# Moving the query transposes, one query load and one value fold inside the queues of a pooled-attention and maxout-FFN kernel

## The chip, the core and the metric

The kernel runs on one core of a Trainium2 chip. The metric is the device time of one execution in microseconds (us). The profile's own clock begins with the first instruction of the span; all times "at 62.28" below are on that clock.

## The reference

```python
# q, k, v: (8 batches, 8 heads, 576 tokens, 64), float32
k_p = k.reshape(B, H, 72, 8, D).mean(axis=3)      # keys and values pooled by 8
v_p = v.reshape(B, H, 72, 8, D).mean(axis=3)
scores = scale * np.matmul(q, k_p.transpose(0, 1, 3, 2))
attn = softmax(scores)                            # exp, divided by the sum
x = np.matmul(attn, v_p)                          # then (8 * 576, 512)
h = np.maximum(np.maximum(x @ w1, x @ w2), x @ w3)   # w: 512 x 768
out = h @ w_out                                   # 4608 x 512, float32
```

## The kernel before

Two kinds of units run side by side. The attention goes by batch: b = 0 to 7, 576 tokens each. The feed-forward part goes by tile of 512 tokens: n = 0 to 8. Since 576 is not 512, the tile n needs rows of two batches: the hidden products of tile 3 need the first three chunks of 128 tokens of batch 3, those of tile 4 the rest of batch 3 and the first two chunks of batch 4, those of tile 5 the rest of batch 4 and the first two chunks of batch 5.

The order of the work is written out by hand. Inside a `manual_schedule`, each engine and each queue does its instructions in the order in which the program records them. `block(n, plan, parts)` records tile n as a row of slots: each slot is one piece of `hidden(n)` (line L335, products with the two stored weight differences) or of `project(n)` (lines L380 and L384, then a copy to `osb` at L389 and two stores by SP at L393). For tiles 2 to 4 the slots 0 to 11 are hidden pieces and 12 to 19 are project pieces. After a slot's own piece, the plan's steps of the attention for that slot are recorded by `do(b, steps)`:

- `k`: the pooled keys `kp` are turned on TensorE (L176) and copied into `kz` (L181).
- `s0` to `s7`: the scores of one head (L194) and their exponentials (L199). They read the turned queries `qT`.
- `v0` to `v4`: the values of one chunk of 128 tokens (L243), and their division by the sums (L249, L251) into `xn`.
- `x0` to `x4`: `xn` is turned into `xT`, which the feed-forward products read. For batches 0 to 2 TensorE does it (L233); from batch 3 on it is a transposing DMA that SP issues (L227).
- `T`: the queries of a whole batch are turned from `qb` into `qT` by one transposing DMA that SP issues (L277). It is used from batch 3 on; batches 0 to 2 are turned on TensorE (L169). Below, T(b) is the one of batch b, and x(b,c) is the transpose of chunk c of batch b.

SP's queue thus holds, in one order, the stores of `project`, the x transposes and the T transposes. An instruction in it that waits holds everything behind it.

POOL (GpSimd) issues all loads of k, v and q from batch 1 on, and it folds k and v: three additions each, from eight rows to one (L138, L139, L141). `pool_work(n)` is recorded at slot 0 of block n. It first issues the loads of batch n + 3, the load of k made to wait for a matmul of that slot by `after(...)`, and then does the folds that `FOLDS_OF[n]` lists. The folds `k2` and `v2` stand between blocks 0 and 1. A load into `qb` waits for the transpose that read the buffer before: the load of q of batch 4 waits for T(3), that of batch 6 for T(4), that of batch 7 for T(5).

Each tag has few buffers: `qb`, `vt` and the later `kt` have two, `qT` has two, `xn` six and `osb` five.

After block 5, `weave()` does the tiles 6 to 8 in another form (products `pA`, `pB`, `pC` at L712) with the scores and values of batches 6 and 7 between them, by a list `ORDER`; its first step turns the keys of batch 7.

Of the kernel before, what the change touches and what calls it, by code (L numbers as in the profile page):

```python
# [14 lines left out]
def kernel(  # L15
# [51 lines left out]
    def after(loads, first):  # L67
        for x in loads:
            tc.add_manual_dep(x.ins, first.ins.name, mybir.DependencyInfo(
                mybir.DependencyClass.Sync, mybir.DependencyReason.DATA),  # L70
                reason="weights first")

    def load_k(b, eng, dtype=F16, parts=1):
        kts[b] = (const if b == 0 else ld).tile([96, 6, POOL, D], dtype,
                                                name=f"kt{b == 0}", tag=f"kt{b == 0}")
        src = k[b].rearrange("h s d -> (h s d)").rearrange(
            "(p i j d) -> p i j d", p=96, i=6, j=POOL)
        n = 6 // parts
        return [eng.dma_start(out=kts[b][:, i:i + n], in_=src[:, i:i + n])
                for i in range(0, 6, n)][-1]  # L80

    def load_v(b, eng, dtype=F16, cuts=(0, H)):
        vts[b] = ld.tile([Sp, H, POOL, D], dtype, name="vt", tag="vt")
        src = v[b].rearrange("h (sp j) d -> sp h j d", j=POOL)
        return [eng.dma_start(out=vts[b][:, h:g], in_=src[:, h:g])
                for h, g in zip(cuts, cuts[1:])][-1]

    def load_q(b):
        qbs[b] = ld.tile([128, 4, NG, D], BF16, name="qb", tag="qb")
        src = q[b].rearrange("h s d -> (h s d)").rearrange(  # L90
            "(hp p t d) -> p hp t d", hp=4, p=128, t=NG)
        n = 2 if b == 0 else 4
        for i in range(0, 4, n):
            nc.gpsimd.dma_start(out=qbs[b][:, i:i + n], in_=src[:, i:i + n])
# [51 lines left out]
    def fold_k(b, e, i0=0, i1=6):  # L146
        if b not in kps:
            new_kp(b)
        fold(e, kts[b][:, i0:i1], kps[b][:, i0:i1], F16 if e is nc.vector else F32)

    def fold_v(b):
        fold(nc.gpsimd, vts[b], vp_all[:, b, :, 0:D])
# [327 lines left out]
    def block(n, plan, parts, folds=()):  # L480

        for slot, _ in enumerate(part for stage in parts for part in stage(n)):
            if slot == 0 and n > 0:
                pool_work(n, mms[-1])
            for b, steps in plan.get(slot, ()):
                if b < B:
                    do(b, steps)
            if folds and slot in FOLDS:
                next(folds.pop(0))
# [14 lines left out]
    def plan1():  # L504
        return {1: [(1, "x2")], 2: [(1, "v4")], 3: [(1, "x3")],
                5: [(1, "x4")],
                6: [(2, "k")], 7: [(2, "q0")], 9: [(2, "q1")], 11: [(2, "q2 s0")],
                12: [(2, "s1 q3")], 13: [(2, "s2")], 14: [(2, "s3")], 15: [(2, "s4")],
                16: [(2, "s5")], 18: [(2, "s7")],
                19: [(2, "v0")],  # L510
                20: [(2, "v1 x0")], 21: [(2, "v2 x1")], 22: [(2, "v3 x2")],
                23: [(2, "v4 x3")], 24: [(2, "x4"), (4, "T")], 17: [(2, "s6"), (3, "T")]}

    def plan(n):
        b = n + 1
        got = {0: [(b, "k")]}
        got.update({2 + h: [(b, f"s{h}")] for h in range(H)})
        got.update({12 + c: [(b, f"v{c} x{c}")] for c in range(5)})
        got[18] = [(b + 2, "T")]
        return got  # L520

    FOLDS_OF = {1: "k3 v3", 2: "k4 v4 k5", 3: "v5 k6", 4: "v6 k7 v7"}

    def pool_work(n, mm):

        if n + 3 < B:
            after([load_k(n + 3, nc.gpsimd)], mm)
            load_v(n + 3, nc.gpsimd)
            load_q(n + 3)
        for name in FOLDS_OF.get(n, "").split():  # L530
            if name[0] == "k":
                fold_k(int(name[1]), nc.gpsimd)
            else:
                fold_v(int(name[1]))
# [227 lines left out]
    def with_keys(n):  # L762
        got = plan(n)
        got[17] = got.get(17, []) + [(n + 2, "k")]
        return got

    folds = [f for wi in range(1, 3) for f in [fold_w(wi)] * 4]
    block(1, plan1(), (hidden, project))
    for n in range(2, 5):
        block(n, with_keys(n) if n == 5 - 1 else plan(n),  # L770
              (hidden, project))
# [50 lines left out]
```

The softmax here doesn't subtract the row's maximum and nothing guards it: scores larger than these inputs give would overflow.

## Time and profile before

| | us |
|---|---|
| median of 3 runs | 234.96 |
| lowest and highest of them | 231.76, 235.74 |
| the profiled execution | 231.92 |
| its span in the profile | 230.2 |
| TensorE (PE) busy in the span | 220.2 |
| POOL busy | 137.9 |
| DVE busy | 128.2 |
| ACT busy | 120.9 |

The profiled execution is one of those near the lowest time. The 1.7 us between its time and its span lie outside the first and the last instruction. An engine's busy time does not count the issuing of DMAs on SP; POOL's issuing of a load, 0.55 to 0.86 us each, is shown in the timeline of POOL. A DMA has two times: how long the issuing queue is held, and when the data has landed, which the trace gives by the semaphores.

### The profile page before, as it was taken

The page shows a single profiled execution, that of the slowest core. Times are in us where ns is not written, and L with a number is a line of the kernel's source. Part 1 is how long each engine was busy: PE and PEld are TensorE (multiplying, and loading weights), DVE is VectorE, ACT ScalarE, POOL GpSimd, SP SyncE. Part 2 cuts the span into 40 slices and gives each one's busy share as a digit, 9 for nine tenths or more (in the row PEclk, how much of TensorE's full clock was granted, in tenths as well). Part 3 has the DMA queues.
Part 4 walks back from the last instruction along what each step waited for, and adds up shares of the span by engine and source line. Part 5 has one row for each costly group of instructions (what it writes and reads, how often), then busy time and mean ns, then how long its engine had stood idle before and what let it go on. Part 6 is the DMA issues. An engine that isn't in the chain of part 4 may idle for free.

```text
span 230.2 us, 4549 instructions
## 1 busy us (share of the span) xinstructions
PE 220.2 (96%) x1766; PEld 137.1 (60%) x1766; DVE 128.2 (56%) x238; ACT 120.9 (53%) x216; POOL 137.9 (60%) x113
## 2 busy tenths in 40 slices
PE   7688999999999999999999999999999999999992
PEld 2466745558756455545554555455678667786682
DVE  3558867037425333633362336278579887897730
ACT  2257534755874577237623762574686535465330
POOL 7665201999927999999995999900243442920020
PEclk9999999999999999999999999999999999999999
DMA  6999999999499889979995999691430536302236
GB/s 180 207 195 197 212 202 211 177 187 219 91 186 165 199 164 167 152 171 184 197 201 119 171 182 223 120 192 33 91 66 17 117 72 99 74 20 46 68 73 182
DMA packets 47173, 33.53 MB, mean 146 GB/s; under 512 B 27312, under 2 KB 41904, under 8 KB 47152
## 3 DMA queue, kind: packets, MB, share of 16 engines
q0 software_dynamic: 16960, 16.98, 46.0%
q1 hardware_dynamic: 30032, 16.13, 32.3%
q8 instruction: 14, 0.23, 0.4%
q10 hardware_dynamic: 160, 0.13, 0.2%
q14 instruction: 7, 0.06, 0.1%
HBM read 34.60 MB, written 9.44 MB: 191 GB/s over the span
## 4 chain that ended last, share of the span: by engine, by line
PE 89%; DMA 4%; DVE 2%; issue 1%; ACT 1%; POOL 1%; POOLq 0%; DVEq 0%
PE pw L335 27%; PE po L384 18%; PE po L380 12%; PE pA L712 7%; PE psc L194 5%; PE pav L243 4%; DMA vt<-in_v_dram 4%; PE pC L712 3%; PE pm L322 2%; PE oA L649 2%; PE pB L712 2%; PE pxt L233 1%; PE pkt L176 1%; DVE xn L251 1%; PE oC L649 1%
## 5 line engine op out<-in xcount | busy, mean ns | idle before, releaser
L335 PE MATMUL pw<-xT,mw 128*128 128x512 f16 (+1 forms) x336 | 73.1, 349 | 0.3 <-ACT xT L237 0.2
L384 PE MATMUL po<-mwo,hT 128*128 128x512 f16 (+1 forms) x198 | 46.8, 372 | 0.0
L343 DVE TENSOR_TENSOR hT<-t,pw 128x512 f16<-128x512 f16 (+1 forms) x42 | 25.5, 609 | 37.2 <-ACT et L199 22.6
L389 ACT COPY osb<-po 128x512 f32<-128x512 f32 (+1 forms) x32 | 18.5, 580 | 42.2 <-PE po L384 40.1
L335 PEld LDWEIGHTS <-mw 128*128 128x128 f16 x336 | 29.0, 98 | 19.5 <-DVE mw L308 0.6
L199 ACT ACTIVATE et<-psc 72x576 f16<-72x576 f32 (+2 forms) x54 | 35.2, 661 | 6.6 <-PE psc L194 6.6
L138 POOL TENSOR_TENSOR half<-vt 72x2048 f32<-72x2048 f16 x7 | 28.4, 4061 | 13.9 <-DMA vt<-in_v_dram 13.6
L380 PE MATMUL po<-wm,xT 128*128 128x512 f16 (+1 forms) x132 | 33.1, 373 | 0.0
L341 ACT ACTIVATE t<-pw 128x512 f16<-128x512 f32 (+1 forms) x42 | 22.6, 537 | 14.8 <-PE pw L335 13.1
L251 DVE TENSOR_TENSOR xn<-pav,rcp 128x512 f16<-128x512 f32 x40 | 27.6, 691 | 1.4
L384 PEld LDWEIGHTS <-hT 128*128 128x128 f16 x198 | 18.4, 98 | 16.2
L139 POOL TENSOR_TENSOR half<-half 72x1024 f32<-72x1024 f32 (+1 forms) x13 | 27.3, 2097 | 1.0
L194 PEld LDWEIGHTS <-kz 128*128 128x128 bf16 x191 | 17.5, 98 | 13.7 <-DVE kz L181 0.4
L194 PE MATMUL psc<-qT,kz 128*128 128x320 bf16 (+2 forms) x168 | 22.4, 246 | 0.4 <-DVE kz L181 0.3
L243 PEld LDWEIGHTS <-et 72*128 72x128 f16 x320 | 15.4, 98 | 7.6 <-issue 0.4
L718 ACT CAST pad<-pA 128x512 f16<-128x512 f32 x27 | 15.3, 587 | 8.5 <-PE pA L712 6.0
L138 POOL TENSOR_TENSOR half<-ktFalse 96x1536 f32<-96x1536 f16 x6 | 18.6, 3096 | 0.3
L249 DVE RECIPROCAL rcp<-pav 128x8 f32<-128x8 f32 x40 | 8.2, 206 | 18.4 <-PE pav L243 18.2
L380 PEld LDWEIGHTS <-xT 128*128 128x128 f16 x132 | 11.9, 98 | 9.0
L243 PE MATMUL pav<-vp,et 72*128 72x65 f16 x320 | 16.9, 194 | 0.2 <-ACT et L199 0.2
L693 DVE SCALAR_TENSOR_TENSOR hT<-pad 128x512 f16<-128x512 f16 x18 | 14.4, 810 | 1.8 <-ACT pad L722 1.4
L712 PEld LDWEIGHTS <-sw 128*128 128x128 f16 x144 | 13.7, 98 | 2.7
(102 smaller groups left out, 273.9 us busy)
## 6 DMA issues: line engine op xcount, KB each, us to landing
out_dram<-osb SPq DMA_DIRECT2D x62, 128.0 KB, 2.5
ktFalse<-in_k_dram POOLq DMA_DIRECT2D x7, 576.0 KB, 6.8
qb<-in_q_dram POOLq DMA_DIRECT2D x7, 576.0 KB, 13.6
vt<-in_v_dram POOLq DMA_DIRECT2D x7, 576.0 KB, 11.4
mw<-in_moe_w_dram POOLq DMA_DIRECT2D x9, 256.0 KB, 9.4
ktTrue<-in_k_dram SPq DMA_DIRECT2D x3, 384.0 KB, 4.9
mwo<-in_moe_w_out_dram POOLq DMA_DIRECT2D x1, 768.0 KB, 13.1
qb<-in_q_dram POOLq DMA_DIRECT2D x2, 288.0 KB, 8.2
```

The source lines that it names most:

```text
L138: e.tensor_tensor(out=f, in0=t[:, :, 0:4, :], in1=t[:, :, 4:8, :], op=ALU.add)
L139: e.tensor_tensor(out=f[:, :, 0:2, :], in0=f[:, :, 0:2, :], in1=f[:, :, 2:4, :], op=ALU.add)
L194: nc.tensor.matmul(out, kz_all[b % 2][:, f % 2, h, :], qTs[b][:, n + i0:n + i1, 64 * (h % 2):64 * (h % 2) + 64], start=True, stop=True)
L199: nc.scalar.activation(out=out, in_=in_, func=FT.Exp, scale=1.0 / 64.0)
L243: nc.tensor.matmul(pav[:, h // 4, 65 * (h % 4):65 * (h % 4) + 65], ets[b][:, h, c0:c0 + 128], vp_all[:, b, h, :], start=True, stop=True)
L251: nc.vector.tensor_tensor(out=xn, in0=pv[:, :, :, 0:D], in1=rcp.to_broadcast([128, 2, 4, D]), op=ALU.mult)
L335: mm = nc.tensor.matmul(pw, w_sb[wi][:, kc, bass.ts(jc, 128)], xT[:, kc, col], start=(kc == 0), stop=(kc == KCH - 1))
L341: nc.scalar.activation(out=t, in_=pw, func=FT.Relu)
L343: nc.vector.tensor_tensor(out=hT[:, jc, c0:c1], in0=t, in1=pw, op=ALU.max)
L380: nc.tensor.matmul(po, xT[:, kc, bass.ts(m, 128)], wm_sb[:, kc, c], start=(kc == 0), stop=False)
L384: nc.tensor.matmul(po, hT[:, jc, bass.ts(mm, 128)], wo_sb[:, jc, c], start=False, stop=(jc == JCH - 1))
L712: mm = nc.tensor.matmul(p[:, w], a[:, kc, bass.ts(g, 128)], b[:, kc, :], start=(i in FIRST and w + kc == 0), stop=(w + kc == 2), skip_grou ...
```

## The change

Three things are moved; nothing is added or taken away.

- T moves in the plans. T(3) is recorded at slot 15 of block 1 in place of slot 17. T(5), T(6) and T(7) were recorded at slot 18 of blocks 2, 3 and 4; now T(5) is recorded at slot 14 of block 2, behind x(3,2), and T(6) and T(7) at slot 13 of blocks 3 and 4, behind x(4,1) and x(5,1). T(4) keeps its slot.
- The load of q of batch 4 (the fifth batch) is issued ahead of the loads of k and v of that batch.
- The fold of v of batch 6 is done at the end of block 3's pool work, and so ahead of the loads of batch 7, which stand at the head of block 4's.

```diff
 def plan1():
         ...
-                12: [(2, "s1 q3")], 13: [(2, "s2")], 14: [(2, "s3")], 15: [(2, "s4")],
+                12: [(2, "s1 q3")], 13: [(2, "s2")], 14: [(2, "s3")], 15: [(2, "s4"), (3, "T")],
         ...
-                23: [(2, "v4 x3")], 24: [(2, "x4"), (4, "T")], 17: [(2, "s6"), (3, "T")]}
+                23: [(2, "v4 x3")], 24: [(2, "x4"), (4, "T")], 17: [(2, "s6")]}

 def plan(n):
         ...
-        got[18] = [(b + 2, "T")]
+        got[14 if n == 2 else 13].append((b + 2, "T"))
         return got

-    FOLDS_OF = {1: "k3 v3", 2: "k4 v4 k5", 3: "v5 k6", 4: "v6 k7 v7"}
+    FOLDS_OF = {1: "k3 v3", 2: "k4 v4 k5", 3: "v5 k6 v6", 4: "k7 v7"}

 def pool_work(n, mm):
         if n + 3 < B:
+            if n == 1:
+                load_q(4)
             after([load_k(n + 3, nc.gpsimd)], mm)
             load_v(n + 3, nc.gpsimd)
-            load_q(n + 3)
+            if n > 1:
+                load_q(n + 3)
```

The recorded order on SP changes accordingly, and by nothing else. T(3) has the same place in SP's queue at either slot, since SP has no other instruction between them.

## The prediction

> **What bounds the kernel now.** I read the page's busy times and slices first, then the busy times by stage, then the waits of PE, then the timelines of POOL and SP in the stages that the change touches.
>
> ```profile
> PE 220.2 (96%) x1766; PEld 137.1 (60%) x1766; DVE 128.2 (56%) x238; ACT 120.9 (53%) x216; POOL 137.9 (60%) x113
> ...
> PE   7688999999999999999999999999999999999992
> ...
> PEclk9999999999999999999999999999999999999999
> DMA  6999999999499889979995999691430536302236
> ```
>
> PE is busy for 96% of the span at the full granted clock. What is missing lies at the two ends. The DMA engines are nearly full until slice 26 (about 150 us), so a transfer there takes as long as its neighbours allow.
>
> The busy times by stage (length, then PE, PEld, DVE, ACT, POOL, clock, DMA share, GB/s) show the blocks 2, 3 and 4:
>
> ```profile
> 78.70:101.50 22.80, 22.80 (x160) 11.80 (x158) 9.37 (x17) 11.28 (x19) 22.16 (x13) 1.00 0.92 164
> 101.50:124.30 22.80, 22.80 (x160) 11.80 (x158) 9.37 (x17) 11.28 (x19) 21.13 (x12) 1.00 0.92 177
> 124.30:147.50 23.20, 23.20 (x165) 12.03 (x164) 10.11 (x18) 11.91 (x20) 21.14 (x11) 1.00 1.01 177
> ```
>
> PE has no idle time in them, POOL very little. The waits of PE between 23 and 216 us are one row of 0.2 us:
>
> ```profile
> PE pw L335 <- ACT xT L237: 0.2, 1, 0.2
> ```
>
> So in this execution nothing that the change touches holds PE. Its parts can only move margins: how long before PE needs a thing it is there.
>
> The timeline of POOL at the loads of batch 4, and at those of batch 7 (start, length, in brackets the idle time before and what ended it):
>
> ```profile
> 63.24 0.57 POOL L79 DMA_DIRECT2D ktFalse<-in_k_dram  x1
> 63.80 0.85 POOL L85 DMA_DIRECT2D vt<-in_v_dram  x1
> 70.11 0.78 POOL L94 DMA_DIRECT2D qb<-in_q_dram  x1 [5.45 <-DMA qT<-qb]
> 70.91 3.11 POOL L138 TENSOR_TENSOR half<-ktFalse 96x1536 f32<-96x1536 f16 x1
> ...
> 125.45 0.55 POOL L79 DMA_DIRECT2D ktFalse<-in_k_dram  x1 [2.25 <-PE pw L335]
> 126.00 0.86 POOL L85 DMA_DIRECT2D vt<-in_v_dram  x1
> 127.20 0.78 POOL L94 DMA_DIRECT2D qb<-in_q_dram  x1 [0.35 <-issue]
> ```
>
> POOL stands 5.45 us in the load of q(4) until T(3) is done, with the fold of k(3) behind it. SP's timeline from block 4:
>
> ```profile
> 127.81 9.67 SPq L277 DMA_TRANSPOSE qT<-qb  x1
> 137.59 1.18 SPq L393 DMA_DIRECT2D out_dram<-osb  x2
> 139.31 1.19 SPq L227 DMA_TRANSPOSE xT<-xn  x1
> ```
>
> T(6) holds SP for 9.67 us. The trace has its data landed 14.2 us after its start; T(4), with no load beside it, took 4.0 us and T(3), issued just before two loads, 7.3 us. So a T beside loads is slow, and all behind it on SP waits.
>
> **The change part by part.** Landings are read from the trace's semaphores.
>
> *q(4) ahead of k(4) and v(4).* The load waits for T(3), issued at 62.28 in both kernels, as soon as q(3) has landed (62.14). If T(3) is as quick as T(4) with the two loads no longer beside it, it lands at 66.3; if they did not slow it, at 69.5 as now. From landing to issue took 0.57 us (69.54 to 70.11). Then come 0.78 + 0.57 + 0.85 us of issues: the fold of k(3) starts at 69.1 or 72.3, in place of 70.91. I take 69.1, since the only difference between T(3) and T(4) that the rows show is the loads. The fold takes 6.06 us (70.91 to 76.97), so the keys are there at 75.1 (or 78.4); PE reaches their transposes at 79.55. The margin goes from 2.6 to 4.4 us (or 1.2). On the path: nothing. Without the cover it would be whatever exceeds that margin. k(4) and v(4) land some 4 to 6 us later (71.4 and 75.2 before), but POOL folds them only from about 85 on. T(4) no longer waits for q(4) (2.9 us of SP before 80.63); its first reader is at 104.4, 20 us later.
>
> *T(5) behind x(3,2).* q(5) landed at 98.32, x(3,2) was issued until 98.83, so T(5) issues without a wait. It adds its 2.2 us of SP ahead of two stores, x(3,3) and x(3,4), which landed by 103.85 and are read at 124.1. x(3,2) itself, which landed at 100.44 for a product at 101.36, has the same place: its margin of 0.9 us stays, or grows, if the loads of batch 5 run 1.8 us earlier with POOL. Nothing on the path.
>
> *T(6) behind x(4,1).* q(6) landed at 120.08 (118.3 with POOL's 1.8 us); x(4,1) was issued until 120.24, so T(6) follows without a wait and ahead of the loads of batch 7. I give it 4.0 us, the far bound is 14.2. It is read at 148.2, so either fits. SP pays 2.2 us in block 3 and gets back 9.67 us in block 4, where x(5,0) was issued only 0.5 us after SP had its stores done (139.31 against 138.77). x(4,2) to x(4,4) go 2 to 4 us later, and are read at 147.4. Nothing on the path.
>
> *v(6) folded ahead of the loads of batch 7.* The fold (128.00 to 135.84) fills the 2.25 us in which POOL waited for PE. k(6) was folded by 123.20, or 121.4 with the gain above; plus 7.8 us the loads start at 129.2, not 125.45. At their old times to landing (6.6, 11.6, 13.7) k(7) lands at 135.8, v(7) at 141.4 and q(7) at 144.4. POOL idles 4.4 us, starts k(7) at 135.9 as before, and PE turns the keys at 160.3. T(7) waits on SP from about 143.2 to 144.4 and holds two stores and x(5,2) behind it; that one belongs to tile 6, whose products begin at 163.1, and T(7)'s data is read at 164.9.
>
> What comes nearer is x(5,1). Hidden(5) reads it at 147.37; it landed at 144.99, 3.1 us after its issue. Now q(7) is still loading then. From the rows, an x took 2.4 us with nothing beside it and 5.1 us (x(3,0)) in the tail of batch 5's loads, so it lands between 144.3 and 147.0. I take 146, as its neighbour x(5,0) took 4.4 beside loads: margin 1.4 in place of 2.4 us. On the path nothing, but the thinnest cover of the change.
>
> The Trainium skill, "DMA: Bandwidth & Descriptors", section "Rules for kernel authors", speaks against this part: a DMA should be issued early and waited for late, and two of the three moves issue loads later. The trace has the load of k(7) used 3.9 us after it landed and its keys needed 18 us after the fold. By the rule the loads' delay of 3.8 us would be lost, 235.7 for the profiled execution; by the rows nothing is.
>
> *T(3) at slot 15:* same place on SP and on PE. Nothing.
>
> **The sum.** Removed from PE's path 0, added 0: 231.92 for an execution like the profiled one. The median, 234.96, is 3.0 us over it, and no trace shows where. Either the 3.0 us are of a kind that the change cushions (T(6) only 2.9 us longer, the 0.5 and 2.4 us above, makes PE wait; 6 us longer explains 3.0), or they lie elsewhere. I take the first, since T's times spread from 4.0 to 14.2 us, wider than any transfer that the change leaves alone: 232.0.
>
> **The rivals.** *The 3 us lie outside: 235.0.* The nearest place is the load of v(1): it landed at 39.31, its fold starts at 39.39, and behind it POOL folds k(2), there at 55.39 for PE at 56.48. That margin of 1.1 us is smaller than those that the change widens, and the change does not touch it. Against it: v(1) would have to land 4.1 us later to cost 3.0.
>
> *Batch 7's loads catch x(5,0) and x(5,1): slower.* T(6) lost 10.2 us (14.2 less 4.0) beside these loads. If x(5,0), issued at 139.3, lost as much, it would land at 151.9 and x(5,1) after it at about 153; PE would stand 5.7 us at 147.4, 240.7 on top of the median. It decides from 147.4 on. Against it: x(3,0) lost only 2.7 us in such a tail.
>
> *Faster by over 2%.* PE's idle before 23 us is out of reach, so below 231 there is little to win; it would take both a kernel before at its upper end (235.74) and one after at 231.0. I price it at 230.2.
>
> **How the numbers follow.** The forecast has 0.43, the outside cause 0.32, the loads on x(5,1) 0.14, faster 0.11. A difference under 2% is about what a measurement of this kernel can tell from no change, so the first two, at 1.3% and 0%, are both "within": 0.75. The range runs from 230.6, where half of the faster case begins, over the first two to 236.8, the upper rival's 235.0 with the scatter of the runs (235.74) and a late x(5,1) of 1 us.
>
> **What would show it.** Right: POOL's wait before q(4) at about 3.6 us counted from 63.2, the k(3) fold starting near 69; T(5), T(6) and T(7) each landing in 4 to 6 us, and no SP entry near 9.7 us; PE without idle from 23 us on. Wrong: T(3) still landing near 69.5; idle time of PE at 147.4 ended by xT; or a median near 235, with the idle ahead of block 2.

## The result, and the profile after

The changed kernel has a median of 231.93 us (231.74 to 232.10, 4 runs), and the kernel before, with one run more than shown above, 233.36 us (231.4 to 235.74). The ratio of after to before is 1.0014, with a 95% interval of 0.9994 to 1.0033: no difference. Two of the runs of before (234.96 and 235.74) lie more than 1.5% above its fastest and are left out of the ratio, as such runs are in every comparison below, so a ratio and the medians beside it need not agree to the last digit. The profiled execution took 232.10 us, its span 230.3 us.

The page after, busy times and slices:

```profile
PE 220.5 (96%) x1766; PEld 137.2 (60%) x1766; DVE 128.2 (56%) x238; ACT 120.8 (52%) x216; POOL 137.7 (60%) x113
...
PE   7778999999999999999999999999999999999992
...
PEclk9999999999999999999999999999999999999999
DMA  6999999989649999996998699961430536301336
```

The same 220 us of PE at the full granted clock. Only the DMA digits have moved: the loads come at other times. By stage (length, then PE, PEld, DVE, ACT, POOL, clock, DMA share, GB/s), PE is again full in blocks 2 to 4, and POOL has the fold of v(6) in block 3 and less to do in block 4 (18.34 us, 21.14 before):

```profile
78.70:101.50 22.80, 22.80 (x160) 11.83 (x159) 9.37 (x17) 11.27 (x19) 22.16 (x13) 1.00 1.17 187
101.50:124.30 22.80, 22.80 (x160) 11.81 (x159) 9.37 (x17) 11.27 (x19) 22.17 (x13) 1.00 0.98 183
124.30:147.50 23.20, 23.20 (x166) 12.00 (x164) 10.12 (x18) 11.90 (x20) 18.34 (x11) 1.00 0.99 167
```

The waits of PE between 23 and 216 us are still one row of 0.2 us:

```profile
PE pw L335 <- ACT xT L237: 0.2, 1, 0.2
```

So nothing was taken from PE's path and nothing put on it. What did move is seen in POOL's timeline (start, length, in brackets the idle time before):

```profile
67.83 0.77 POOL L94 DMA_DIRECT2D qb<-in_q_dram  x1 [3.92 <-DMA qT<-qb]
68.60 0.55 POOL L79 DMA_DIRECT2D ktFalse<-in_k_dram  x1
69.14 0.85 POOL L85 DMA_DIRECT2D vt<-in_v_dram  x1
70.00 3.10 POOL L138 TENSOR_TENSOR half<-ktFalse 96x1536 f32<-96x1536 f16 x1
...
130.12 0.56 POOL L79 DMA_DIRECT2D ktFalse<-in_k_dram  x1
...
136.70 3.08 POOL L138 TENSOR_TENSOR half<-ktFalse 96x1536 f32<-96x1536 f16 x1 [4.39 <-DMA ktFalse<-in_k_dram]
```

and in SP's (start and the time for which the queue is held):

```profile
77.70 6.22 SPq L277 DMA_TRANSPOSE qT<-qb  x1
...
98.99 2.56 SPq L277 DMA_TRANSPOSE qT<-qb  x1
...
120.72 2.27 SPq L277 DMA_TRANSPOSE qT<-qb  x1
...
143.59 2.92 SPq L277 DMA_TRANSPOSE qT<-qb  x1
```

T(6) no longer holds SP for 9.67 us but for 2.27. But T(4), which took 1.89 us of SP before, now holds it for 6.22: the loads of k(4) and v(4) are still under way when it is issued (they land at 78.04 and 84.02). The jam has changed place, and at neither place does PE wait for what is behind it.

### The profile page after: what moved, and what is told of

Same layout as the page of the kernel before. It is cut to its first block, busy times and chain, and to the rows that moved or that the text cites. A ratio compares the mean times of both kernels' runs of the same rounds, so it can differ in the third digit from the quotient of the medians.

```text
span 230.3 us, 4548 instructions
## 1 busy us (share of the span) xinstructions
PE 220.5 (96%) x1766; PEld 137.2 (60%) x1766; DVE 128.2 (56%) x238; ACT 120.8 (52%) x216; POOL 137.7 (60%) x113
## 4 chain that ended last, share of the span: by engine, by line
PE 89%; DMA 4%; DVE 2%; issue 1%; ACT 1%; POOL 1%; POOLq 0%; DVEq 0%
PE pw L335 27%; PE po L384 18%; PE po L380 12%; PE pA L715 7%; PE psc L194 5%; PE pav L243 4%; DMA vt<-in_v_dram 4%; PE pC L715 3%; PE pm L322 2%; PE oA L652 2%; PE pB L715 2%; PE pxt L233 1%; PE pkt L176 1%; DVE xn L251 1%; PE oC L652 1%
## 5 line engine op out<-in xcount | busy, mean ns | idle before, releaser
L380 PE MATMUL po<-wm,xT 128*128 128x512 f16 (+1 forms) x132 | 33.0, 372 | 0.0
L380 PEld LDWEIGHTS <-xT 128*128 128x128 f16 x132 | 11.9, 98 | 9.0
```

The source lines that it names most:

```text
L380: nc.tensor.matmul(po, xT[:, kc, bass.ts(m, 128)], wm_sb[:, kc, c], start=(kc == 0), stop=False)
```

## The experiments

Two theories were tested. The first: PE's own work is the length of the kernel from 23 us on, both kernels meet it with margins of 0.4 us and more, and the change only moves the margins. The second: the jams on SP, or POOL's order, are a cost of the kernel before in its usual executions, which the change takes away.

**How much room is there at x(3,2)?** T(5) goes ahead of it instead of behind it.

```diff
-        got[14 if n == 2 else 13].append((b + 2, "T"))
+        got[13].append((b + 2, "T"))
```

> The changed kernel, but T(5) one slot earlier, ahead of x(3,2) on SP in place of behind it. Theory 1 (the changed kernel is bound by PE alone, and x(3,2), landed at 100.97 for a product at 101.4, has a margin of about 0.4 us): T(5) waits for q(5) (98.9), holds SP about 2.3 us, x(3,2) lands at 103.7 to 104.9, PE stands 2.3 to 3.5 us ahead of block 3's first products; 1.0 to 1.5% over the changed kernel. Rival (hidden(3) does not read that chunk first, or the DMA engines take the two transposes side by side): under 0.7 us.

Median 233.25 us (12 runs) against 231.60 of before, ratio 1.0051 (1.0022 to 1.0080). PE's timeline at the head of block 3:

```profile
100.29 0.59 PE L384 MATMUL po<-mwo,hT 128*128 128x512 f16 x2
102.24 0.59 PE L335 MATMUL pw<-xT,mw 128*128 128x512 f16 x2 [1.36 <-ACT osb L389]
```

The profile puts the idle 1.36 us down to a copy by ACT, but x(3,2) landed at 102.15, just before PE goes on. The place was right and the size, 2.3 to 3.5 us, too large: q(5) landed 1.6 us earlier here (97.27) than in the first profile after, so T(5) waited less. One slot on SP is worth about half a per cent here (1.3 us over the changed kernel's 231.93).

**How much at x(5,1)?** T(7) goes ahead of it.

```diff
-        got[14 if n == 2 else 13].append((b + 2, "T"))
+        got[{2: 14, 3: 13, 4: 12}[n]].append((b + 2, "T"))
```

> The changed kernel, but T(7) one slot earlier, ahead of two stores and of x(5,1). Theory 1: T(7) waits for q(7) (143.5), holds SP until 146, x(5,1) is issued at 147.4 and lands at about 150.5, PE, which reaches hidden(5) at 147.4, stands 3 to 4.5 us; 1.3 to 1.9% over. It would show that of the move of the loads only the margin of x(5,1) counts. Rival (q(7) lands earlier now that nothing follows it on SP, or PE has other work): under 1 us.

Median 235.19 us (12 runs), ratio 1.0111 (1.0072 to 1.0151). PE at the head of block 5, and SP with the reason (T(7) waits for q(7), x(5,1) is in the row of two behind the stores):

```profile
150.59 0.38 PE L335 MATMUL pw<-xT,mw 128*128 128x512 f16 x1 [3.34 <-DMA xT<-xn]
```

```profile
138.94 1.21 SPq L227 DMA_TRANSPOSE xT<-xn  x1
143.71 1.96 SPq L277 DMA_TRANSPOSE qT<-qb  x1
145.77 2.03 SPq L393 DMA_DIRECT2D out_dram<-osb  x2
147.89 2.56 SPq L227 DMA_TRANSPOSE xT<-xn  x2
```

The 3.34 us idle are as expected, and the median is 3.3 us over the changed kernel's 231.93. But the two numbers don't belong together: the profiled run, at 237.16 us, is one of the longer ones, and its span is 5.0 us over that of the changed kernel. The rest is in the granted clock, the share of full speed that PE was given. After the wait it is 0.50 for 3.41 us:

```profile
151.04:154.45 3.41, 3.41 (x12) 1.51 (x11) 0.00 (x0) 1.13 (x2) 0.00 (x0) 0.50 0.57 123
```

Half of 3.41 us is 1.7, and 3.34 + 1.7 = 5.0. So a wait of PE can cost more than its length. An order on SP that is wrong by one slot costs what the margin does not hold.

**How much did T(6)'s old place have?** T(6) is issued twice, in the kernel before and in the changed one. The second writes the same data.

```diff
+                for _ in range(2 if b == 6 else 1):
                     nc.sync.dma_start_transpose(
```

> The kernel before, with T(6) issued twice over (the second writes the same data and waits for the first). Theory 1 (SP's order is what ties T(6) to PE, with 2.9 us of cushion behind it): the second T(6) runs from 142 to 144.3, x(5,1) is issued at 148.2 to 149 and lands at 150.7 to 152, PE stands 3 to 4.5 us; 1.3 to 2%. Rival (T(6) has more cushion than that, so it can't have cost the 3 us in the median of before): under 1 us.

Median 238.76 us (6 runs), ratio 1.0263 (1.0197 to 1.0330). In the profile (the copied lines stand one lower here):

```profile
103.20 1.02 PE L336 MATMUL pw<-xT,mw 128*128 128x512 f16 x4 [2.09 <-DMA xT<-xn]
...
153.88 0.59 PE L336 MATMUL pw<-xT,mw 128*128 128x512 f16 x1 [4.50 <-DMA xT<-xn]
```

4.50 us at hidden(5) is the upper end of the expected wait. As in the experiment above, 3.41 us at a granted clock of 0.50 follow it (153.88 to 157.29), another 1.7 us, which the expectation did not count. The 2.09 us at hidden(3) come ahead of T(6), so the edit did not make them: in this execution T(3) landed at 71.25 (69.54 in the first profile), the loads of batch 5 started 1.7 us later, and x(3,0) to x(3,2) took 8.8, 7.1 and 5.7 us beside them. The margin of 0.9 us at x(3,2) was used up by a POOL that was late 30 us earlier.

> The changed kernel, with T(6) issued twice over. Theory 1: T(6) now stands in block 3, the second one holds SP about 4 us more there, x(4,2) to x(4,4) land at about 130 to 135 and are read at 147.4: 0 us, the same time as the changed kernel. Rival (the stores and transposes pushed behind it run into the loads of batch 7 and x(5,0), x(5,1) come late): 1 us or more.

Median 233.17 us (12 runs), ratio 1.0040 (1.0000 to 1.0081). The rival was right here: PE stood 2.25 us at hidden(5).

```profile
149.41 0.38 PE L336 MATMUL pw<-xT,mw 128*128 128x512 f16 x1 [2.25 <-DMA xT<-xn]
```

The second T(6) pushed x(4,3) to 128.9, into the first of the loads of batch 7. It took 10.6 us to land, x(5,1) then 7.9 (149.28). So the changed kernel's order does bear a late T(6) better than the old one (0.4% against 2.6%, of which the profile puts 2.09 us at hidden(3) and 1.7 us on the clock), but not for nothing.

**Is PE the bound?** Half of the products of line L380 are left out in tile 3, 1.73 us of PE.

```diff
-                for kc in range(KCH):
+                for kc in range(2 if n == 3 else KCH):
```

> The changed kernel with half of the products of xT and wm left out in tile 3 (8 matmuls of 0.216 us, 1.73 us of PE in block 3, where nothing waits). Theory 1 (PE's own work is the whole length from 23 us on): 1.5 to 1.75 us less than the changed kernel, 0.7% under it. Rival (a queue or a transfer that PE merely meets on time sets the pace in blocks 3 and 4, x(4,1) with 2 us and x(5,1) with 0.7 us of margin): under 1 us less, and new idle time of PE at hidden(4) or hidden(5).

Median 230.42 us (9 runs), ratio to before 0.9954 (0.9932 to 0.9977). The changed kernel had 231.93 and, later, 231.48, so 1.1 to 1.5 us of the 1.73 came out, a little less than theory 1 asked for. The profile, of one of the longer runs (231.67 us), has the new idle time that the rival named: PE arrives early at hidden(5) and waits there.

```profile
146.76 0.59 PE L335 MATMUL pw<-xT,mw 128*128 128x512 f16 x2 [1.35 <-DMA xT<-xn]
```

PE is the bound, and the x transposes of batch 5 beside batch 7's loads are the next one, less than 1 us behind (the margin of 0.7 us of x(5,1) in the changed kernel).

**The parts alone**, each against the kernel before:

```diff
 # load of q(4) alone: load_q(4) ahead of load_k, load_v for n == 1
 # T alone:
-        got[18] = [(b + 2, "T")]
+        got[14 if n == 2 else 13].append((b + 2, "T"))
 # v(6) alone:
-    FOLDS_OF = {..., 3: "v5 k6", 4: "v6 k7 v7"}
+    FOLDS_OF = {..., 3: "v5 k6 v6", 4: "k7 v7"}
```

(T(3)'s move from slot 17 to 15 changes no queue and is not in these kernels.)

> The kernel before with only the load of q(4) moved ahead of k(4) and v(4). Theory 1: POOL waits about 3.9 us in place of 5.45 in the load of q(4), the fold of k(3) starts about 1 us earlier, T(4) on SP is held about 6 us by the two loads that now run beside it, T(6) is held about 9.7 us as before; PE idle as before, 0 us. Rival (T(4)'s jam is a cost that the other parts make good): 1 us or more.

Median 231.54 us, ratio 0.9983 (0.9957 to 1.0009). T(4) held SP for 4.8 us and T(6) for 9.6, and between 23 and 216 us PE waited for nothing but the same 0.2 us: the jams are real and free.

```profile
77.59 4.79 SPq L277 DMA_TRANSPOSE qT<-qb  x1
...
127.70 9.59 SPq L277 DMA_TRANSPOSE qT<-qb  x1
```

```profile
PE pw L335 <- ACT xT L237: 0.2, 1, 0.2
```

> The kernel before with only the T transposes moved. Theory 1: T(5) and T(6) land about 4 us after their issue and hold SP about 2.3 us, T(7) follows x(5,1) at 143.2 with q(7) landed at about 141; the loads of batch 7 start at 125.5 as before, x(5,1) lands at about 144.5 to 145.5; PE idle as before, 0 us. Rival (the moves are what keeps the time from getting worse): a difference of 1 us or more either way.

Median 231.97 us, ratio 1.0027 (1.0007 to 1.0046). In the profile T(5) and T(6) landed 4.1 and 4.2 us after their issue, x(5,1) at 145.63, and PE did not wait: as expected. The interval lies just above 1, so this part alone is, if anything, 0.3% longer; its profile shows no place for it.

> The kernel before with only the fold of v(6) moved ahead of the loads of batch 7. Theory 1 (T(6) was slow because of the loads beside it): the loads start at about 131, T(6), issued at 127.8, holds SP for 2 to 3 us in place of 9.67 and lands in 4 to 5.5 us; x(5,1) lands at 146.5 to 147.4, so 0 to 0.5 us more. Rival (T(6) is slow there because of the stores just ahead of it on SP): T(6) holds SP 6 us or more.

T(6), at 127.0, held SP for 1.97 us and landed in 4.0, with the loads from 130.3 on: it was the loads that slowed it.

```profile
127.03 1.97 SPq L277 DMA_TRANSPOSE qT<-qb  x1
```

But the median was 233.61 us (8 runs), ratio 1.0100 (1.0074 to 1.0125), 2 us more where 0 to 0.5 were expected, while the profile (231.07 us) had no wait and x(5,1) at 145.95. So pairs of parts were run.

> The kernel before with the load of q(4) moved and the fold of v(6) moved, the T transposes left. If what the fold of v(6) costs alone (2 us in the timed runs) is batch 7's loads reaching x(5,0) and x(5,1), and the load of q(4) makes it good by running POOL about 1 us earlier: loads from about 130, x(5,1) landing at about 146.5, 231.5 to 232.5 us. Rival (the T moves make it good, by taking T(6) and the stores behind it off the loads): about 233.5 us as with v(6) alone.

> The kernel before with the T transposes moved and the fold of v(6) moved, the load of q(4) left. If POOL's 1 us matters: loads of batch 7 from about 131, x(5,1) late by 0 to 2 us, 232.5 to 234 us, as with v(6) alone. Rival (the T moves make it good): 231.5 to 232.3 us.

With the load of q(4): 231.47 us (231.1 to 231.6), ratio 0.9982 (0.9951 to 1.0013). With the T moves: 232.11 us (230.98 to 233.62), ratio 1.0024 (0.9979 to 1.0069). The order of the two medians fits POOL's microsecond as the remedy, but the intervals overlap, and the profiles don't show it: x(5,1) landed at 145.99 and 145.79 us, against 145.95 with v(6) alone.

> The fold of v(6) moved alone, once more, beside the next kernel on the same chip: its first profile showed no wait of PE while its timed runs were 2 us longer. If the cost is batch 7's loads reaching x(5,0) and x(5,1): about 233 us, and if the profile falls on a long run, idle time of PE at hidden(5) (about 147) ended by xT, x(5,1) landing after it. Rival (another place): idle time elsewhere, or none.

On another chip v(6) alone had 232.27 us and a ratio of 1.0006 (0.9969 to 1.0042): the 1% did not come again. Its profile (233.30 us) shows where such a run loses time. Of the waits of PE from 100 to 200 us:

```profile
PE pw L335 <- DMA xT<-xn: 1.6, 1, 1.6
```

x(5,0) and x(5,1) took 7.1 and 7.0 us beside batch 7's loads; x(5,1) landed at 148.49, 0.25 us before PE goes on at hidden(5).

> As the one beside it, but the load of q(7) is issued only after the fold of k(7) (about 143), so x(5,0) and x(5,1) meet the loads of k(7) and v(7) alone, which land by about 140. If the cost is these loads on the two transposes: both take 2.5 to 3.5 us, x(5,1) lands at 144 to 145, 231.3 to 231.9 us, 2 us under the kernel beside it. T(7) waits on SP for q(7) until about 151, used at 165, which costs nothing. Rival: about 233 us as the kernel beside it.

231.92 us, ratio 0.9983 (0.9951 to 1.0015), not separated from the kernel beside it. x(5,0) took 2.4 us as expected, but x(5,1) 4.6, with q(7)'s load now starting just behind it. So the place of v(6)'s cost is seen in one profile, and whether it has a cost in most executions stays open (1.0% on one chip, none on another).

**What would the rival "outside" cost?** One spare POOL addition of 4.06 us after the fold of v(1), in the kernel before:

```diff
     fold_v(1)
+    nc.gpsimd.tensor_tensor(out=spare, in0=vts[1][:, :, 0:4, :], in1=vts[1][:, :, 4:8, :],
+                            op=ALU.add)
```

> The kernel before with one spare POOL addition (4.06 us, the first step of a fold, done once more, its result unused) between the fold of v(1) and the loads of batch 3. It prices the rival that 3 us of the median lay outside the change: k(2) is folded 4.1 us later, at 59.5 for PE at 56.5: PE stands 3.0 us there (2.5 to 3.5), 1.3% over; k(3) comes 4.1 later too, at 81, against a PE that is itself 3 us late (82.6), so no second wait. Rival (POOL's chain has more cushion there): under 1 us.

Median 236.28 us (6 runs), ratio 1.0187 (1.0145 to 1.0228):

```profile
59.13 0.44 PE L176 MATMUL pkt<-ident,kp 96*64 96x96 bf16 x6 [3.59 <-POOL kp L141]
```

The wait at k(2) is there, 3.59 us for 3.0 expected, and x(5,1) makes a second one of 2.07 us at hidden(5), which was not expected:

```profile
152.59 0.67 PE L335 MATMUL pw<-xT,mw 128*128 128x512 f16 x2 [2.07 <-DMA xT<-xn]
```

After the second wait the granted clock is 0.50 for 3.41 us once more (152.96 to 156.37); after the first, which was longer, it stays at 1.00. The profiled run is the longest of the six (238.77 us), so whether the others have the second wait is open; the median's 4.2 to 4.7 us over before are more than the first alone, and the other five runs too were granted a little less of the clock (0.985 to 0.996) than the changed kernel beside them (0.997 to 1.0).

**The changed kernel beside the parts.**

> The changed kernel as it is, on the chip and beside the runs of the parts, to set the parts and the kernel with less PE work against it. Theory 1: 231.6 to 232.1 us, no difference from before beyond 0.2%. Rival (its margin of 0.7 us at x(5,1) is used up in part of the runs, as with v(6) alone): a median of 232.5 us or more.

Median 231.48 us (231.1 to 233.02, 6 runs), ratio 0.9996 (0.9958 to 1.0034): no difference, as theory 1 has it, 0.1 us under its range.

## Why the prediction was right and wrong

*Right: the sum.* "Removed from PE's path 0, added 0: 231.92 for an execution like the profiled one." It took 232.10 us, and no part alone gained more than its interval. Of the signs named for being right, POOL's wait (3.9 us for 3.6), the landings of T(5), T(6) and T(7) (4.1, 4.0 and 5.0 us), no SP entry near 9.7 us and a PE without idle all came, and no time was gained: they could test the sum, not the step behind it.

*Wrong: the last step, from the sum to the forecast.* The prediction noted that the median of 234.96 stood 3.0 us over the profile and that "no trace shows where", and then took it as something "that the change cushions". That made a forecast of 1.3% less out of a sum of nothing, by a term of 3.0 us that no row of the profile held. The runs show in its place that the median of before had nothing to give: beside the experiments it was 231.60 (29 runs), 231.61 (25), 232.09 (11) and 232.00 us (23), so the 3.0 us belonged to two of its first three runs. That the forecast of 232.0 us lies beside the measured 231.93 is luck: it was reached by taking 3.0 us off a median that stood 3 us too high. What makes single runs long stays open: 14 of those 88 runs of before took over 234 us and none of the ten of the changed kernel, but ten are too few to tell, and no trace of a long run of before was kept. A kernel of which two of three runs lie high and whose one profile lies low had told that its median was not to be trusted, and the sum was to be held against the low runs: ratio 1.00. The reason given was that T's times spread wider than those of any transfer that the change leaves alone. That was not so in the trace at hand (the loads of v(2) and v(3), which are left alone, took 24.8 and 10.8 us), and it said nothing on PE: with the load of q(4) alone, T(6) still holds SP for 9.6 us and PE has no wait. The tie itself was real: with T(6) issued twice, SP was held until 146.85 in place of 137.48, and PE stood 4.5 us at hidden(5). The rival "outside" kept the same 3 us and fell with them; its place, at k(2), does have the small margin that it named, as the spare addition shows.

*The load of q(4).* T(3) without loads beside it was priced at 4.0 us and took 4.06. The fold of k(3) started at 70.00; the prediction's 69.1 with q(3) landing 0.95 us later in this execution gives 70.05. Right. For the same reason the margin of the keys is 3.6 us (there at 76.05, read at 79.61), not 4.4.

*T(4): missed.* That it would not wait for q(4) was right (73.5). That the loads of k(4) and v(4), moved behind q(4), would run beside it was not counted: it held SP for 6.22 us and landed in 8.3, not about 4. The two loads themselves came 6.6 and 8.8 us later than before, for "some 4 to 6". All this was free, with T(4)'s reader at 104.4.

*x(3,2).* "Its margin of 0.9 us stays, or grows" was wrong in sign: it landed at 100.97, about 0.45 us ahead of its product. POOL's issues came 0.9 us earlier, but v(4), which had been expected by about 81, landed at 84.0, so the loads of batch 5 finished later (98.86 for 98.32).

*T(6) and v(6).* T(6): 4.04 us for 4.0. Loads of batch 7 at 130.1 for 129.2, POOL's idle 4.39 us for 4.4, q(7) at 143.5 for 144.4. The prediction had set against this part the rule to issue a DMA early and wait for it late (the Trainium skill, "DMA: Bandwidth & Descriptors", section "Rules for kernel authors"). The loads went out 4.7 us later than before (130.12 for 125.45), and in the profile after PE did not wait. What the later loads cost where they cost something, in the second profile with v(6) alone, was 1.6 us by way of x(5,1), not a delay of 3.8.

*x(5,1), "the thinnest cover of the change".* Expected at 146 within 144.3 to 147.0, it landed at 146.72 for PE at 147.43: a margin of 0.7 us for 1.4 expected and 2.4 before. The rival on x(5,0) and x(5,1) was right in its place: the changed kernel with T(6) twice, the one with less PE work and v(6) alone (in its second profile) all have their wait there. Its price, 5.7 us, was not reached; these waits are 1.35 to 2.25 us.

## What to carry to other kernels

Where the engine that bounds the kernel has no idle time in the profile, freeing a queue or another engine can't shorten it; such a change trades margins, and each margin is to be written down as "landed at, needed at". When a median stands over its one profile and no row shows why, it should not be turned into a gain: hold the sum against the runs that look like the profile. A load that is moved changes every transfer that it now meets, so a jam that leaves one transpose should be looked for at the next. In this case a query transpose issued ahead of the loads left its queue after about 2 us, one issued behind them after 4.8 or more. And a wait of the bounding engine should be priced with what the granted clock does behind it.

## What was not expected of the hardware

How long a query transpose holds SP goes by whether a load was under way when it was issued. In the sixteen traces of this case, the 13 T transposes that were issued with a load of k, v or q still in flight held SP for 4.8 to 12.1 us, and the 69 others for 1.8 to 3.2. A load that is issued just behind a T makes its data late but does not hold the queue: T(3) before held SP for 2.0 us and landed in 7.3, T(5) with the load of q(4) alone for 2.2 and landed in 10.3. In 12 of the 13 the hold ended within 0.3 us of the landing of v's load. SP's own stores just ahead are not what decides: in the kernel with the spare POOL addition, T(5) was issued 0.1 us behind the load of k(6), with stores ahead of it that took 2.3 and 2.4 us.

```profile
106.75 10.65 SPq L277 DMA_TRANSPOSE qT<-qb  x1
```

What makes the queue wait was not tried. The x transposes, 2.3 to 2.5 us when alone, took up to 10.6 us beside the start of the loads of batch 7.

A wait of PE brought a stretch at half the clock in three of the traces: 3.41 us at 0.50, after waits of 3.34, 4.50 and 2.07 us. It did not after five waits of 1.35 to 2.25 us, nor after the 3.59 us at k(2). So the length of the wait alone does not decide it, and no run here was made to find what does.
